# Split attention and a max-out FFN on one core: one ring of four PSUM banks, V loaded by half sequence, masks by a compare, a regrouped first FFN chunk

## The chip, the cores and the metric

The kernel runs on one core of a Trainium2 chip. TensorE (PE in the profile) multiplies matrices and transposes; its weight loads are listed apart as PEld. VectorE (DVE), ScalarE (ACT) and GpSimd (POOL) do elementwise work; In this kernel whatever leaves PSUM goes through DVE or ACT. SyncE (SP) issues most DMAs. The metric is device time in microseconds, the median of several executions of the whole kernel. Every engine works through its own instructions strictly in program order, and semaphores tie the engines together: an instruction that waits holds back all that stands behind it on its engine.

## The reference

Attention over 4 batches, 8 heads, 768 positions and a head width of 64, followed by a feed-forward network (FFN) with a maximum of three projections. Some heads ("retrieval" heads, by a flag in the input) see all earlier positions; the others see the first 4 positions and a window of 64.

```python
scores = q @ k.T / sqrt(64)                   # per batch and head, 768 x 768
mask = causal if is_retrieval[h] else causal & (first 4 positions | last 64)
a = softmax(where(mask, scores, -1e9))
x = (a @ v)  -> [4*768, 8*64]                 # heads side by side
h = maximum(maximum(x @ w1, x @ w2), x @ w3)  # 512 -> 768
out = h @ w_out                               # 768 -> 512, float32
```

## The kernel before, in words

The work is cut into 32 steps. Step `s` is one batch, one half of the sequence (384 query positions) and one pair of heads; four steps in a row (the four head pairs) make one half, eight steps one batch. A step of the first half has 6 blocks of 128x128 scores a head, a step of the second half has 15. The instructions are issued in the order in which the Python loop writes them (`manual_schedule`); no planner moves them.

For each step the loop does this, and the names in brackets are those of the profile:

- `load(s)`: SP loads K, Q and V of the step (`ks`, `qs`, `vs`), seven steps ahead.
- `prep(s)`: DVE casts K to fp16 (`kn`, L268), ACT casts Q (`qn`, L269). `prep_v(s)`: V is cast into a store of all heads (`va`, by ACT in the first four steps, by DVE later, L281), and POOL writes a second store `vf` (L283) in which the far positions of non-retrieval heads are zeroed.
- `turn(s)`: PE transposes K and Q into one PSUM tile (`tr`, L296), DVE copies it out (`KQ`, L303).
- `scores(s, units)`: PE multiplies K by Q into PSUM (`st`, two buffers of two banks each, L324), ACT takes the exponential (`pt`, L334), POOL multiplies the blocks on the diagonal and next to it by masks (`mk`, L356). A first-half step has two units, a second-half step four: `[0, 1]` at the step's start, `[2, 3]` later in it.
- `av(s)`: PE multiplies the exponentials by V (`oacc`, L371; a column of ones in V gives the softmax sum); DVE takes the reciprocal (`rc`, L379) and multiplies (`x`, L381).
- `turn_x(s)`: PE transposes `x` (`tr`, L396), DVE copies it out (`xT`, L399).

When the four head pairs of a half are done, `ffn(b, half)` is queued. It is a generator of 24 units. Eighteen units are four matmuls each over 384 positions into PSUM (`yy`, L219), for six blocks of the 768 columns and three weights: the first weight's product is copied by ACT into `acc` (L227), the second and the third are compared with it by DVE (`acc`, then `hT`, L230). The last six units are three products with `w_out` (`yy`, L237; each is counted as two), copied by ACT (`ot`, L244) and stored by SP (L246). The units of one half are spread over the steps that follow it: `share` issues some of them at three points of every step. The last half's units have no steps left and stand at the end.

PSUM has eight banks. Before the change four belong to `st`, one to `oacc`, one to `tr` (shared by `turn` and `turn_x`), two to `yy`. A tile that takes a buffer of its pool waits until the reader of that buffer's last tile has finished. `yy` therefore waits for the reader of the `yy` two units earlier; `tr` waits for the copy of the `tr` before it.

The masks `mk` of the eight heads are built at the start, per head pair, by a DVE instruction with two SBUF inputs (L175). The seven loads of the weights are issued by POOL after step 1.

Of the kernel before, what the change touches and what calls it, by code (L numbers as in the profile page):

```python
# [48 lines left out]
def kernel(  # L49
# [54 lines left out]


    staged = {}

    def load(s):
        b, half, hp = where(s)
        hs, ts = slice(2 * hp, 2 * hp + 2), slice(half * HALF, (half + 1) * HALF)  # L110
        t = []
        for nm, src in (("ks", k), ("qs", q), ("vs", v)):
            st = stage.tile([P, 2, HB, D], FP32, tag=nm, name=nm)
            if nm == "vs":
                for hl in range(2):
                    nc.sync.dma_start(
                        out=st[:, hl],
                        in_=src[b, 2 * hp + hl, ts].rearrange("(j p) d -> p j d", p=P),
                    )
            else:  # L120
                nc.sync.dma_start(
                    out=st, in_=src[b, hs, ts].rearrange("h (p j) d -> p h j d", p=P)
                )
            t.append(st)
        staged[s] = t

    ir32 = consts.tile([P, 2 * H], mybir.dt.int32, name="ir32")
# [4 lines left out]
    for s in range(AHEAD):  # L132
        load(s)
# [14 lines left out]
    W = consts.tile([P, 512], FP16, name="W")  # L148
    nc.gpsimd.affine_select(
        out=W[:, 0:256], in_=base, compare_op=ALU.is_gt, fill=0.0,  # L150
# [4 lines left out]
    nc.vector.tensor_copy(out=W[:, 256:512], in_=W[:, 0:256])  # L155
    if n_sink > 0:
        nc.vector.tensor_copy(out=W[0:n_sink, 256:512], in_=base[0:n_sink, :])
    F = consts.tile([P, 512], FP16, name="F")
    for c in (0, 256):
        nc.vector.tensor_tensor(  # L160
            out=F[:, c : c + 256], in0=base, in1=W[:, c : c + 256], op=ALU.subtract
        )
    RT = consts.tile([P, H], FP32, name="RT")
    nc.vector.tensor_copy(out=RT, in_=ir32[:, 0 : 2 * H : 2])

    far = consts.tile([P, H, 4], FP16, name="far")
    nc.vector.tensor_copy(out=far, in_=RT.unsqueeze(2).to_broadcast([P, H, 4]))
    if n_sink > 0:
        nc.vector.memset(far[0:n_sink, :, 0:1], 1.0)

    mk = consts.tile([P, H, 512], FP16, name="mk")

    def head_masks(hp):
        for h in (2 * hp, 2 * hp + 1):
            nc.vector.scalar_tensor_tensor(  # L175
                out=mk[:, h], in0=F, scalar=RT[:, h : h + 1], in1=W,
                op0=ALU.mult, op1=ALU.add,
            )

# [4 lines left out]

    w_t = [consts.tile([P, KS, DF], FP16, name=f"w{wi}t") for wi in range(3)]
    woutt = consts.tile([P, NNB, DMdl], FP16, name="woutt")

    def load_weights():
        for c in (0, DF // 2):
            for wt, w in zip(w_t, (moe_w1, moe_w2, moe_w3)):  # L190
                nc.gpsimd.dma_start(
                    out=wt[:, :, c : c + DF // 2],
                    in_=w[:, c : c + DF // 2].rearrange("(ks p) n -> p ks n", p=P),
                )
        nc.gpsimd.dma_start(
            out=woutt, in_=moe_w_out.rearrange("(ns p) m -> p ns m", p=P)
        )
# [4 lines left out]
    def ffn(b, half):  # L202
# [3 lines left out]
        def psum():  # L206
            nonlocal n_yy
            n_yy += 1
            if last and n_yy % 2:
                return sps.tile([P, 2, 512], FP32, tag="st", name="yst")[:, 0, :]  # L210
            return fsp.tile([P, 512], FP32, tag="fsp", name="yy")

        hT = [htp.tile([P, HALF], FP16, tag=f"hT{n}", name=f"hT{n}") for n in range(NNB)]
        for ni in range(NNB):
            acc = None
            for wi in range(3):
                yy = psum()
                for ks in range(KS):
                    nc.tensor.matmul(  # L219
                        yy[:, 0:HALF],  # L220
                        w_t[wi][:, ks, ni * P : (ni + 1) * P],
                        xT[b, half][ks],
                        start=(ks == 0), stop=(ks == KS - 1),
                    )
                if wi == 0:
                    acc = fwork.tile([P, HALF], FP16, tag="acc", name="acc")
                    nc.scalar.copy(out=acc, in_=yy[:, 0:HALF])  # L227
                else:
                    dst = acc if wi == 1 else hT[ni]
                    nc.vector.tensor_tensor(  # L230
                        out=dst, in0=yy[:, 0:HALF], in1=acc, op=ALU.max
                    )
                yield
# [30 lines left out]
    def prep(s):  # L264
        qs, ks_ = staged[s][1], staged[s][0]
        qn = half16.tile([P, HB, 2, D], FP16, tag="qn", name="qn")
        kn = half16.tile([P, HB, 2, D], FP16, tag="kn", name="kn")
        nc.vector.tensor_copy(out=kn, in_=ks_.rearrange("p h j d -> p j h d"))  # L268
        nc.scalar.copy(out=qn, in_=qs.rearrange("p h j d -> p j h d"))  # L269
        cast[s] = (kn, qn)  # L270

    def prep_v(s):
        b, half, hp = where(s)
        vs = staged.pop(s)[2]
# [3 lines left out]
        if s < NHP:  # L278
            nc.scalar.copy(out=vdst, in_=vs)
        else:  # L280
            nc.vector.tensor_copy(out=vdst, in_=vs)  # L281
        k1 = min(k0 + HB, 4)
# [8 lines left out]
    def turn(s):  # L291
        tr = trp.tile([P, 1024], FP16, tag="tr", name="tr")
# [17 lines left out]
    def scores(s, us):  # L310
# [21 lines left out]
        for u, st in zip(us, sts):  # L332
# [4 lines left out]
            for at, u0, nu, cols, n, m0 in MASKED[half]:  # L337
                if at != u:
                    continue
                for hl_all in (slice(0, 2),):  # L340
# [15 lines left out]
                    nc.gpsimd.tensor_tensor(out=x, in0=x, in1=m, op=ALU.mult)  # L356
# [3 lines left out]
    def av(s):  # L360
        b, half, hp = where(s)
        pt, j = pts.pop(s), b % 2
        o = ops.tile([P, HB, 2, VW], FP32, tag="oacc", name="oacc")
# [23 lines left out]
    def turn_x(s):  # L387
# [6 lines left out]
        tr = trp.tile([P, 1024], FP16, tag="tr", name="tr")  # L394
# [8 lines left out]

    FIRST = NHP + 1
    weight = [0 if s < FIRST else (5, 7)[where(s)[1]] for s in range(NSTEP)] + [3]
    units = (2 * B - 1) * 24
    emitted = 0

    def share(s, part, parts):
        nonlocal emitted  # L410
        if s > NSTEP:
            return
        want = units * (sum(weight[:s]) + weight[s] * (part + 1) / parts) / sum(weight)
        n = int(want + 1e-6) - emitted
        if n > 0:
            fill(n)
            emitted += n

    head_masks(0)
    prep(0)  # L420
    turn(0)
    head_masks(1)
    prep(1)
    prep_v(0)
    for s in range(NSTEP + 2):
# [62 lines left out]
```

## Time and profile before

| | |
|---|---|
| median of 3 runs | 243.78 us (243.57 to 244.28) |
| the profiled execution | 244.76 us, of which the span of the profile is 243.1 us |
| PE busy | 206.3 us (85%), weight loads 122.2 us (50%) |
| DVE / ACT / POOL busy | 147.4 (61%) / 132.0 (54%) / 128.5 us (53%) |
| granted TensorE clock | 1.0 throughout |
| moved by DMA | 28.65 MB, mean 118 GB/s |

Three stretches follow each other in the profile: a start in which the first five steps run without any FFN (until 35 us), the body in which steps and FFN units alternate (until about 222 us), and the end with the last half's FFN alone. In the answers quoted below a row of a timeline gives the start in microseconds, how long the group took, engine, line, operation, what it writes and reads, the number of instructions, and in square brackets how long the engine stood idle before it and what ended that.

### The profile page before, as it was taken

The numbers are of one execution on the slowest core, as the hardware profiler recorded it, in microseconds if no ns is written. First come the engines' busy times: TensorE is split into PE (matmuls) and PEld (weight loads), VectorE is DVE, ScalarE is ACT, GpSimd is POOL, SyncE is SP. The second block draws the span as 40 slices with busy tenths as digits, with TensorE's granted clock in tenths as the row PEclk, the third lists the DMA queues.
The fourth block names the chain that finished last, engine by engine and source line by source line (L and its number), as shares of the span: only waits on it lengthen the run. The fifth ranks groups of instructions, "written<-read, shape, count | busy, mean of one in ns | idle before, by whom it ended". The sixth has DMA issues, their size and how long they took to land.

```text
span 243.1 us, 5176 instructions
## 1 busy us (share of the span) xinstructions
PE 206.3 (85%) x2000; PEld 122.2 (50%) x2000; DVE 147.4 (61%) x302; ACT 132.0 (54%) x206; POOL 128.5 (53%) x144
## 2 busy tenths in 40 slices
PE   0455389999998999898988999898989999889993
PEld 0234256655654555564645555564545455555551
DVE  4696545665587736755687546764787646542550
ACT  3564273675643486656644497465535676643222
POOL 2599981655776455437776264528775166441000
PEclk9999999999999999999999999999999999999999
DMA  5999999951892039102783059003300020002103
GB/s 149 282 281 250 207 214 217 253 131 49 253 260 62 3 118 266 39 0 74 230 228 90 3 171 251 3 0 113 116 4 0 27 106 0 3 0 89 46 0 129
DMA packets 50584, 28.65 MB, mean 118 GB/s; under 512 B 27264, under 2 KB 47488, under 8 KB 50560
## 3 DMA queue, kind: packets, MB, share of 16 engines
q1 hardware_dynamic: 46464, 25.18, 37.8%
q0 software_dynamic: 3952, 3.15, 8.1%
q8 instruction: 15, 0.25, 0.4%
q14 instruction: 9, 0.07, 0.1%
q10 hardware_dynamic: 144, 0.01, 0.0%
HBM read 25.17 MB, written 6.29 MB: 129 GB/s over the span
## 4 chain that ended last, share of the span: by engine, by line
PE 48%; DVE 16%; ACT 9%; POOL 9%; issue 8%; DMA 6%; SPq 3%; POOLq 0%; DVEq 0%; ACTq 0%
PE yy L219 19%; PE yy L237 9%; POOL pt L356 7%; PE oacc L371 7%; ACT pt L334 6%; PE st L324 4%; DVE kn L268 4%; DMA ks<-in_k_dram 3%; PE tr L296 3%; DVE acc L230 3%; PE yst L219 2%; DMA qs<-in_q_dram 2%; DVE va L281 2%; DVE mk L175 2%; ACT acc L227 2%
## 5 line engine op out<-in xcount | busy, mean ns | idle before, releaser
L356 POOL TENSOR_TENSOR pt<-pt,mk 128x512 f16<-128x512 f16 (+1 forms) x96 | 101.6, 1081 | 78.4 <-ACT pt L334 78.3
L334 ACT ACTIVATE pt<-st 128x1024 f16<-128x1024 f32 x96 | 83.0, 918 | 42.7 <-PE st L324 34.6
L230 DVE TENSOR_TENSOR acc<-yy,acc 128x384 f16<-128x384 f32 x45 | 25.0, 555 | 26.9 <-PE yy L219 13.5
L219 PE MATMUL yy<-xT,w0t 128*128 128x384 f16 x180 | 37.7, 330 | 3.8 <-DVE acc L230 3.6
L219 PE MATMUL yy<-xT,w2t 128*128 128x384 f16 x180 | 37.2, 330 | 4.2 <-ACT acc L227 4.2
L219 PE MATMUL yy<-xT,w1t 128*128 128x384 f16 x180 | 37.3, 330 | 2.5 <-ACT acc L227 1.7
L227 ACT CAST acc<-yy 128x384 f16<-128x384 f32 x45 | 21.7, 482 | 32.5 <-PE yy L219 28.1
L303 DVE COPY KQ<-tr 128x768 f16<-128x768 f16 x32 | 30.5, 954 | 14.0 <-PE tr L296 14.0
L324 PE MATMUL st<-KQ 64*128 64x384 f16 (+2 forms) x320 | 29.9, 297 | 4.9 <-DVE KQ L303 3.6
L237 PE MATMUL yy<-woutt,hT 128*128 128x512 f16 x132 | 32.5, 379 | 0.5 <-DVE acc L230 0.4
L371 PEld LDWEIGHTS <-pt 128*128 128x128 f16 x672 | 26.3, 100 | 7.2 <-POOL pt L356 3.5
L371 PE MATMUL oacc<-va,pt 128*128 128x65 f16 x352 | 26.7, 199 | 2.9 <-POOL pt L356 2.8
L230 DVE TENSOR_TENSOR hT<-yy,acc 128x384 f16<-128x384 f32 x45 | 25.0, 555 | 5.8 <-PE yy L219 3.5
L283 POOL TENSOR_TENSOR vf<-va,far 128x390 f16<-128x390 f16 (+1 forms) x32 | 20.7, 648 | 11.9 <-DVE va L281 6.0
L219 PEld LDWEIGHTS <-w2t 128*128 128x128 f16 x192 | 17.9, 98 | 16.0 <-issue 6.9
L219 PEld LDWEIGHTS <-w1t 128*128 128x128 f16 x192 | 17.9, 98 | 15.6 <-issue 6.4
L219 PEld LDWEIGHTS <-w0t 128*128 128x128 f16 x192 | 17.8, 99 | 14.9 <-issue 5.7
L244 ACT COPY ot<-yy 128x512 f32<-128x512 f32 x22 | 13.1, 594 | 21.2 <-PE yy L237 21.2
L399 DVE COPY xT<-tr 128x384 f16<-128x384 f16 x32 | 11.4, 356 | 19.9 <-PE tr L396 19.6
L296 PE MATMUL tr<-ident,kn 128*128 128x128 f16 x96 | 11.7, 237 | 13.4 <-DVE kn L268 8.1
L324 PEld LDWEIGHTS <-KQ 64*128 64x128 f16 x320 | 11.9, 98 | 20.3 <-issue 11.2
L371 PE MATMUL oacc<-vf,pt 128*128 128x65 f16 x320 | 21.7, 194 | 0.0
(44 smaller groups left out, 165.4 us busy)
## 6 DMA issues: line engine op xcount, KB each, us to landing
ks<-in_k_dram SPq DMA_DIRECT2D x32, 192.0 KB, 4.0
qs<-in_q_dram SPq DMA_DIRECT2D x32, 192.0 KB, 4.1
vs<-in_v_dram SPq DMA_DIRECT2D x64, 96.0 KB, 3.9
out_dram<-ot SPq DMA_DIRECT2D x24, 256.0 KB, 2.1
w0t<-in_moe_w_dram POOLq DMA_DIRECT2D x2, 384.0 KB, 10.9
w1t<-in_moe_w_dram POOLq DMA_DIRECT2D x2, 384.0 KB, 13.0
w2t<-in_moe_w_dram POOLq DMA_DIRECT2D x2, 384.0 KB, 15.2
woutt<-in_moe_w_out_dram POOLq DMA_DIRECT2D x1, 768.0 KB, 23.2
```

The lines of the kernel that those rows point to most:

```text
L219: nc.tensor.matmul(yy[:, 0:HALF], w_t[wi][:, ks, ni * P : (ni + 1) * P], xT[b, half][ks], start=(ks == 0), stop=(ks == KS - 1),)
L227: nc.scalar.copy(out=acc, in_=yy[:, 0:HALF])
L230: nc.vector.tensor_tensor(out=dst, in0=yy[:, 0:HALF], in1=acc, op=ALU.max)
L237: nc.tensor.matmul(yo[:, 0:DMdl], hT[ns][:, tb * P : (tb + 1) * P], woutt[:, ns, :], start=(ns == 0), stop=(ns == NNB - 1),)
L244: nc.scalar.copy(out=ot, in_=yo[:, 0:DMdl])
L283: nc.gpsimd.tensor_tensor(out=vf[j][:, hs, k0:k1, 0 : D + 1], in0=va[j][:, hs, k0:k1, 0 : D + 1], in1=far[:, hs, k0:k1].unsqueeze(3).to_br ...
L296: nc.tensor.transpose(tr[:, c : c + P], x[:, j].rearrange("p h d -> p (h d)"), ident)
L303: nc.vector.tensor_copy(out=KQs[s].rearrange("p (i t j) -> p i t j", i=2, j=HB), in_=tr[:, 0:S].rearrange("p (i j t) -> p i t j", i=2, j=HB),)
L324: nc.tensor.matmul(st[:, hl, c0 : c0 + n * P], KT[ki // HB if half else 0][hb : hb + D, ki % HB * P : (ki % HB + 1) * P], KQ[hb : hb + D, ...
L334: nc.scalar.activation(out=pt[:, u, :, 0:w], in_=st[:, :, 0:w], func=AF.Exp, scale=sc)
L356: nc.gpsimd.tensor_tensor(out=x, in0=x, in1=m, op=ALU.mult)
L371: nc.tensor.matmul(o[:, qi, hl, 0 : D + 1], pt[:, u, hl, c : c + P], vv[:, 2 * hp + hl, ki, 0 : D + 1], start=(idx == 0), stop=(idx == len ...
```

## The change

1. **PSUM.** The pools of `oacc`, `tr` and `yy` become one pool of four banks (`bank(...)`) that is taken in turn: every new `tr`, `oacc` or `yy` waits for the reader of the tile four places earlier in program order. `st` keeps its four banks. `acc` gets a pool of seven buffers.
2. **Order within a step.** `share` issues its units after `turn_x`, after `av` and at the step's end (before: after `turn_x`, between `turn` and `av`, at the end). In steps 1 to 4 `turn_x` of the step before comes right after `av` in the same step, ahead of the next scores. The 24 units of a half are now dealt out over exactly four steps: 5, 5, 6, 8 units in the steps 9 to 12 and 6, 6, 7, 5 in the steps 13 to 16, and so on (before: about 5 in a first-half step, 7 in a second-half step).
3. **V.** One group of three DMAs of 256 KB loads V of all eight heads for one half (at the load of its second head pair), instead of two DMAs of 96 KB in every step. In the first four steps ACT issues the DMAs of Q.
4. **Masks.** One tile `kept` holds 0, 1 or 2 for every place; a head's mask is `kept > least`, a compare with one SBUF input (L197). In the first four steps the mask of unit 1 is applied by DVE, no longer by POOL. The flags and masks come after the first `turn`.
5. **First FFN.** `ffn(0, 0)` runs by weight: six blocks with `w1`, six with `w2`, six with `w3`. The weights are loaded whole, one in each of the steps 0 to 3, in four DMAs.
6. `vf` is written for one block in the first half and three in the second (before three and one).

The diff, cut to what the prediction speaks of:

```diff
+    accp = ctx.enter_context(tc.tile_pool(name="accp", bufs=7))
-    ops = ctx.enter_context(tc.tile_pool(name="ops", bufs=1, space=bass.MemoryType.PSUM))
-    trp = ctx.enter_context(tc.tile_pool(name="trp", bufs=1, space=bass.MemoryType.PSUM))
-    fsp = ctx.enter_context(tc.tile_pool(name="fsp", bufs=2, space=bass.MemoryType.PSUM))
+    bkp = ctx.enter_context(tc.tile_pool(name="bkp", bufs=4, space=bass.MemoryType.PSUM))
+    def bank(shape, dtype, name):
+        return bkp.tile(shape, dtype, tag="bank", name=name)
...
-        for nm, src in (("ks", k), ("qs", q), ("vs", v)):
+        for nm, src in (("ks", k), ("qs", q)):
+            eng = nc.scalar if s < NHP and nm == "qs" else nc.sync
...
+        if hp == 1:
+            vs = stage.tile([P, H, HB, D], FP32, tag="vs", name="vs", bufs=3)
+            for j in range(HB):
+                r0 = half * HALF + j * P
+                nc.sync.dma_start(
+                    out=vs[:, :, j], in_=v[b, :, r0 : r0 + P].rearrange("h p d -> p h d")
+                )
...
-            nc.vector.scalar_tensor_tensor(
-                out=mk[:, h], in0=F, scalar=RT[:, h : h + 1], in1=W,
-                op0=ALU.mult, op1=ALU.add,
-            )
+            nc.vector.tensor_scalar(
+                out=mk[:, h], in0=kept, scalar1=least[:, h : h + 1], scalar2=None,
+                op0=ALU.is_gt,
+            )
...
+        order = [(wi, ni) for ni in range(NNB) for wi in range(3)]
+        if (b, half) == (0, 0):
+            order.sort()
+        for wi, ni in order:
+            yy = psum()
...
-                    nc.gpsimd.tensor_tensor(out=x, in0=x, in1=m, op=ALU.mult)
+                    eng = nc.vector if s < NHP and u == 1 else nc.gpsimd
+                    eng.tensor_tensor(out=x, in0=x, in1=m, op=ALU.mult)
...
-        if s > 1:
+        if s > FIRST:
             turn_x(s - 2)
-        share(s, 1, 7)
+        share(s, 0, 3)
         if s + 1 < NSTEP:
             turn(s + 1)
-        share(s, 3, 7)
         if 0 < s <= NSTEP:
             av(s - 1)
+        if 0 < s < FIRST:
+            turn_x(s - 1)
+        share(s, 1, 3)
         if s + 2 < NSTEP:
             prep(s + 2)
         if live and n_u > 2:
             scores(s, [2, 3])
         if s + 1 < NSTEP:
             prep_v(s + 1)
-        if s + 2 < NHP:
-            head_masks(s + 2)
-        share(s, 6, 7)
-        if s == 1:
-            load_weights()
+        if 0 < s < NHP - 1:
+            head_masks(s + 1)
+        share(s, 2, 3)
+        if s < 4:
+            load_weight(s)
```

Where the instructions move is seen in three places. The first is DVE at the start, from the first `kn` on. Before:

```order
L268 CAST kn<-ks 128x384
L303 COPY KQ<-tr 128x768
L175 SCALAR_TENSOR_TENSOR mk<-F,RT,W 128x512 x2
L268 CAST kn<-ks 128x384
L303 COPY KQ<-tr 128x768
L268 CAST kn<-ks 128x384
L175 SCALAR_TENSOR_TENSOR mk<-F,RT,W 128x512 x2
L303 COPY KQ<-tr 128x768
```

With the change:

```order
L197 TENSOR_SCALAR mk<-kept,least 128x512 x2
L376 TENSOR_TENSOR pt<-pt,mk 128x2x256
L322 COPY KQ<-tr 128x768
L287 CAST kn<-ks 128x384
L376 TENSOR_TENSOR pt<-pt,mk 128x2x256
L322 COPY KQ<-tr 128x768
L399 RECIPROCAL rc<-oacc 128x6
L401 TENSOR_TENSOR x<-oacc,rc 128x384
L419 COPY xT_266<-tr 128x384
```

A mask product on `pt` (it waits for the exponentials of its step) now stands ahead of the copy `KQ` for the next step's scores.

The second place is ACT at the start. Before:

```order
L128 DMA ir_96<-in_is_retrieval_dram 128x16
L138 ACT_TABLE_LOAD
L138 ACTIVATE warm<-warm 128x2
L269 CAST qn<-qs 128x384 x2
L279 CAST va_171<-vs 128x2x3x64
L334 ACTIVATE pt<-st 128x1024
```

With the change:

```order
L120 DMA qs<-in_q_dram 128x2x192
L136 DMA ir_97<-in_is_retrieval_dram 128x16
L120 DMA qs<-in_q_dram 128x2x192 x3
L146 ACT_TABLE_LOAD
L146 ACTIVATE warm<-warm 128x2
L288 CAST qn<-qs 128x384 x2
L298 CAST va_147<-vs 128x2x3x64
L353 ACTIVATE pt<-st 128x1024
```

The cast `va` of step 0 stands ahead of the first exponential in both; with the change it reads a `vs` that three DMAs of 256 KB fill, the third of which is the fifth DMA on SP.

The third place is DVE in a first-half step of the body (step 10, from its `xT` on). Before:

```order
L399 COPY xT_1105<-tr 128x384
L230 TENSOR_TENSOR hT_1015<-yy,acc 128x384
L303 COPY KQ<-tr 128x768
L379 RECIPROCAL rc<-oacc 128x6
L381 TENSOR_TENSOR x<-oacc,rc 128x384
L268 CAST kn<-ks 128x384
L281 CAST va_172<-vs 128x2x3x64
L230 TENSOR_TENSOR acc<-yy,acc 128x384
L230 TENSOR_TENSOR hT_1016<-yy,acc 128x384
```

With the change:

```order
L419 COPY xT_1065<-tr 128x384
L249 TENSOR_TENSOR hT_974<-yy,acc 128x384
L322 COPY KQ<-tr 128x768
L399 RECIPROCAL rc<-oacc 128x6
L401 TENSOR_TENSOR x<-oacc,rc 128x384
L249 TENSOR_TENSOR acc<-yy,acc 128x384
L249 TENSOR_TENSOR hT_975<-yy,acc 128x384
L287 CAST kn<-ks 128x384
L300 CAST va_148<-vs 128x2x3x64
```

The two maxima, which free banks of `yy`, now stand ahead of the casts `kn` and `va`, which free none.

More of the change, by code (lines that the diff above doesn't have):

```diff
@@ L131 @@
     )
-    for s in range(AHEAD):
+    for s in range(1, AHEAD):
         load(s)
@@ L273, in prep_v @@
         b, half, hp = where(s)
[L274 removed]
+        vs = staged_v[b, half]
         j, k0 = b % 2, half * HB
@@ L362, in av @@
         pt, j = pts.pop(s), b % 2
-        o = ops.tile([P, HB, 2, VW], FP32, tag="oacc", name="oacc")
+        o = bank([P, HB, 2, VW], FP32, "oacc")
         todo = [
@@ L404 @@
     FIRST = NHP + 1
-    weight = [0 if s < FIRST else (5, 7)[where(s)[1]] for s in range(NSTEP)] + [3]
-    units = (2 * B - 1) * 24
-    emitted = 0
     def share(s, part, parts):
-        nonlocal emitted
-        if s > NSTEP:
+        if s < FIRST or s > NSTEP:
             return
[L413 to L419, printed above, removed]
+        s0 = s - (s - FIRST) % NHP
+        ws = [(5, 7, 6)[where(i)[1] if i < NSTEP else 2] for i in range(s0, s0 + NHP)]
+        at = s - s0
+        before, now = (
+            24 * (sum(ws[:at]) + ws[at] * x / parts) / sum(ws) for x in (part, part + 1)
+        )
+        if (part, at) == (parts - 1, NHP - 1):
+            now = 24
+        fill(int(now + 1e-6) - int(before + 1e-6))
     prep(0)
     turn(0)
+    head_flags()
+    head_masks(0)
+    prep(1)
     head_masks(1)
-    prep(1)
     prep_v(0)
```

130 lines of the change are left out of this document (66 added, 64 removed).

## The prediction

> **What bounds the kernel now.** I read first the page's busy times, then the table of windows: one batch of the body, and the body from step 9 on.
>
> ```profile
> PE 206.3 (85%) x2000; PEld 122.2 (50%) x2000; DVE 147.4 (61%) x302; ACT 132.0 (54%) x206; POOL 128.5 (53%) x144
> ...
> 74.82:128.30 53.48, 49.47 (x500) 29.18 (x500) 34.52 (x72) 31.89 (x50) 30.02 (x33) 1.00 0.41 117
> 63.40:221.90 158.50, 145.99 (x1480) 86.27 (x1479) 101.47 (x213) 92.20 (x144) 87.02 (x93) 1.00 0.31 90
> ```
>
> The window's columns are length, then PE, weight loads, DVE, ACT and POOL with their instructions, granted clock, DMA share, GB/s. A batch of eight steps takes 53.48 us; the body holds 158.5/53.48 = 2.96 of them. PE is the busiest engine, but the busy time overstates pipelined matmuls, so I take start-to-start distances from PE's timeline: a second-half step that begins without a stall, then the kinds of stall.
>
> ```profile
> 95.66 0.61 PE L324 MATMUL st<-KQ 64*128 64x384 f16 x8
> 96.21 0.34 PE L396 MATMUL tr<-ident,x 128*128 128x128 f16 x3
> 96.39 0.81 PE L219 MATMUL yy<-xT,w2t 128*128 128x384 f16 x4
> 97.03 0.81 PE L219 MATMUL yy<-xT,w0t 128*128 128x384 f16 x4
> 97.69 0.33 PE L296 MATMUL tr<-ident,kn 128*128 128x128 f16 x3
> ...
> 98.02 0.81 PE L219 MATMUL yy<-xT,w1t 128*128 128x384 f16 x4
> ...
> 99.32 0.23 PE L371 MATMUL oacc<-vf,pt 128*128 128x65 f16 x2
> ...
> 100.35 0.55 PE L324 MATMUL st<-KQ 64*128 64x384 f16 x6
> 100.84 0.82 PE L219 MATMUL yy<-xT,w0t 128*128 128x384 f16 x4
> ...
> 102.94 0.81 PE L219 MATMUL yy<-xT,w2t 128*128 128x384 f16 x4 [0.62 <-ACT acc L227]
> ...
> 72.87 0.81 PE L219 MATMUL yy<-xT,w2t 128*128 128x384 f16 x4
> 74.82 0.48 PE L219 MATMUL yy<-xT,w0t 128*128 128x384 f16 x2 [1.14 <-DVE acc L230]
> ...
> 112.39 0.50 PE L324 MATMUL st<-KQ 64*128 64x384 f16 x6
> 112.82 0.34 PE L396 MATMUL tr<-ident,x 128*128 128x128 f16 x3
> 113.61 0.33 PE L296 MATMUL tr<-ident,kn 128*128 128x128 f16 x3 [0.45 <-DVE xT L399]
> ```
>
> One FFN unit costs PE 0.65 (96.39 to 97.03); an output product, six matmuls of 512 columns instead of four of 384, 0.65 x 6/4 x 512/384 = 1.30. A second-half step's attention costs 0.55 (95.66 to 96.21) + 0.18 + 0.33 (97.69 to 98.02) + 1.03 (99.32 to 100.35) + 0.49 = 2.58. A first-half step has 0.43 (112.39 to 112.82) for scores, the same transposes, and 12 instead of 30 value products, 0.41: 1.35. A batch is 36 x 0.65 + 6 x 1.30 + 4 x 2.58 + 4 x 1.35 = 46.9. So PE loses 6.6 of 53.48 us, nearly all of it waiting for a bank: `yy` for the reader two units back (102.94 instead of 102.14; 74.82 instead of 73.52), `tr` for the copy of the `tr` before (113.61 instead of 113.00).
>
> **The change part by part.** *The ring.* Behind 74.82 stands this piece of DVE's timeline:
>
> ```profile
> 71.54 0.95 DVE L303 COPY KQ<-tr 128x768 f16<-128x768 f16 x1
> 72.42 0.20 DVE L379 RECIPROCAL rc<-oacc 128x6 f32<-128x6 f32 x1
> 72.65 0.56 DVE L381 TENSOR_TENSOR x<-oacc,rc 128x384 f16<-128x384 f32 x1
> 73.12 0.54 DVE L268 CAST kn<-ks 128x384 f16<-128x384 f32 x1
> 73.58 0.72 DVE L281 CAST va<-vs 128x384 f16<-128x384 f32 x1
> 74.22 0.54 DVE L230 TENSOR_TENSOR acc<-yy,acc 128x384 f16<-128x384 f32 x1
> ```
>
> The maximum that frees the bank stood behind `kn` and `va`, 1.26 us. It now stands ahead of them, and the bank is asked for two tiles later. These stalls go; what is late next I find by walking a step with the rows above and these means of one batch:
>
> ```profile
> L230 DVE TENSOR_TENSOR hT<-yy,acc 128x384 f16<-128x384 f32 x12 | 6.6, 554 | 1.3 <-PE yy L219 0.9
> L281 DVE CAST va<-vs 128x384 f16<-128x384 f32 x8 | 3.2, 402 | 0.0
> L399 DVE COPY xT<-tr 128x384 f16<-128x384 f16 x8 | 2.9, 356 | 5.0 <-PE tr L396 5.0
> L334 ACT ACTIVATE pt<-st 128x1024 f16<-128x1024 f32 x16 | 16.0, 1028 | 8.2 <-PE st L324 5.5 <-POOL vf L283 1.4 <-POOL pt L356 1.3
> L227 ACT CAST acc<-yy 128x384 f16<-128x384 f32 x12 | 5.8, 484 | 7.4 <-PE yy L219 7.4
> L269 ACT CAST qn<-qs 128x384 f16<-128x384 f32 x8 | 4.2, 521 | 0.0
> L334 ACT ACTIVATE pt<-st 128x768 f16<-128x768 f32 x4 | 3.2, 807 | 0.0
> L356 POOL TENSOR_TENSOR pt<-pt,mk 128x512 f16<-128x512 f16 x20 | 22.9, 1152 | 21.4 <-ACT pt L334 21.4
> ```
>
> *First-half steps.* DVE does `xT`, `KQ`, `rc`, `x`, `kn`, `va` = 0.36 + 0.95 + 0.20 + 0.56 + 0.54 + 0.40 = 3.0, and two maxima for every three units. Steps 9 and 10 have 5 units: 3.0 + 1.85 and, as an estimate, 0.25 between ten instructions = 5.1, against PE's 1.35 + 3.25 = 4.6. DVE becomes their bound: 5.1 and 5.1, with 6 units 5.5. Step 16 has mostly output products, which ACT copies: PE's 4.6 and a little, 4.9.
>
> *Second-half steps.* Here ACT comes to bind. Scores need a pair of banks that the exponential two units back has read. With two units behind `[2, 3]` (1.3 us; before, three) the next step's scores are there before the last exponential (0.81) is through, and wait. From those scores on PE does the rest of them 0.3, transposes 0.18, two units 1.3, `tr` 0.33, `oacc` 1.03, two units 1.3 = 4.4; ACT then casts `acc` (0.48) and `qn` (0.52) ahead of the exponentials, 1.03 and 0.81. With 0.8 between the step's first two score units, a period of 7.4 comes out, where PE's own work with 6 units is 2.58 + 3.9 = 6.5. Steps 13 and 14 take 7.4 each; step 15, 7 units, 8.0; step 12, 8 units, PE's 7.8.
>
> The batch becomes 5.1 + 5.1 + 5.5 + 7.8 + 7.4 + 7.4 + 8.0 + 4.9 = 51.2, 2.3 less; over 2.96 batches **-6.8**. Bounds: 47.5 a batch if all stalls but small gaps go, 53.5 if DVE and ACT hold PE as before.
>
> *The start.* Rows of the first steps, the price of a DVE product, and the first window:
>
> ```profile
> 9.05 1.51 ACT L334 ACTIVATE pt<-st 128x1024 f16<-128x1024 f32 x2 [0.71 <-PE st L324]
> ...
> 12.63 0.82 PE L324 MATMUL st<-KQ 64*128 64x384 f16 x6 [1.05 <-DVE KQ L303]
> 28.01 1.04 PE L324 MATMUL st<-KQ 64*128 64x384 f16 x8
> 35.05 1.48 PE L219 MATMUL yy<-xT,w0t 128*128 128x384 f16 x4
> ...
> L160 DVE TENSOR_TENSOR F<-base,W 128x256 f16<-128x256 f16 x2 | 0.5, 272 | 0.0
> ...
> 0.00:10.00 10.00, 1.64 (x12) 0.84 (x12) 6.00 (x16) 3.87 (x7) 3.02 (x10) 1.00 0.78 201
> ```
>
> Ahead of ACT's first exponential stands `va`, which now needs V of all heads, 768 KB, with 6 x 192 KB of K and Q on the way: 1.9 MB, at the first window's 201 GB/s 9.6 us. `va` then ends near 10.2 and the exponentials near 11.8, 1.2 later than now. Behind them stand the mask on DVE (two pieces like L160, 0.55; at most POOL's 1.15) and `KQ`: scores of step 1 at about 13.6 instead of 12.63. From there each step is a chain: 0.65 from scores to exponentials (as at 12.63), both 1.51, mask 0.55, `KQ` 0.95, `rc` and `x` 0.76, transposes 0.5 = 4.9. Step 4 comes at 13.6 + 3 x 4.9 = 28.3, now 28.01. The old head masks and the queue of seven weight loads leave DVE and POOL; I count nothing, since the chain does not pass through them. From step 4 to the first FFN unit I keep the 7.0 of the rows. **+0.3**, between -3 and +4.
>
> One row speaks against a mask on DVE: POOL's `vf` took 1.27 while DVE built masks, 0.83 without.
>
> ```profile
> 8.42 1.27 POOL L283 TENSOR_TENSOR vf<-va,far 128x390 f16<-128x390 f16 x1 [5.86 <-DVE KQ L303]
> 13.00 0.83 POOL L283 TENSOR_TENSOR vf<-va,far 128x390 f16<-128x390 f16 x1
> ```
>
> The Trainium skill (SBUF — State Buffer, "Who interferes with whom") says that a DVE instruction with two SBUF inputs contends with a GpSimd instruction that reads SBUF and that the later one waits; by that rule the mask would wait too, and the sum would be higher by up to the rows' 0.44 in each of four steps, 1.8 us.
>
> *The rest.* The first FFN by weight gives ACT six casts in step 5: 3 x 1.03 + 0.81 + 0.52 + 6 x 0.48 = 7.3, no more than the 7.4 above; DVE gets six maxima in steps 6 and 7: 3.0 + 3.3 = 6.3, hidden under the same. 0. `vf` changes places between the halves: 0, since POOL is idle 23 of 53 us. The last FFN keeps its own order: 0. V's DMAs move the same bytes under a body with a DMA share of 0.31; without that cover each group would cost like the first, 1.2.
>
> Sum against the profiled execution: 244.76 - 6.8 + 0.3 = 238.3. The median lies 0.98 below that execution: **237 us**.
>
> **The rivals.** *The ring frees everything* (0.17): 47.5 a batch, -17.7 in all: 226. For it: DVE and ACT are busy only 34.5 and 31.9 us of a batch. Against it: the walk meets both at fixed points of every step.
>
> *PE waits for POOL's masks* (0.13, slower): `oacc` now stands two units, 1.3 us, closer behind the scores `[2, 3]`, whose last two masks take 2.3 behind the exponential of unit 2. PE has 0.49 + 1.3 + 0.55 + 0.18 + 1.3 + 0.33 = 4.15 from those scores to `oacc`; exponential and masks need 0.35 + 1.03 + 2.3 = 3.7. The margin is 0.45. Were the masks slowed as `vf` was (1.27/0.83), they would take 1.2 more, and PE would wait 0.8 in each of four steps: the batch is 51.2 + 3.2 = 54.4, and the sum 244.76 + 0.9 x 2.96 + 0.3 - 0.98 = 247. It decides from 2.3/4 = 0.6 a step, where the gain is gone.
>
> *The limits stay* (0.08): ACT and DVE, not the banks, already hold PE, and the batch stays at its 53.48: 244. Against it: the two stalls above end at the reader of a bank two units back.
>
> *The start pays* (0.07): the bound of +4 is due: 237 + 3.7 = 241; with half the body's gain as well, no gain is left.
>
> The forecast, 231 to 242 by itself: 0.55.
>
> **How the numbers follow.** A measurement of this kernel tells about 0.3%, 0.7 us, from no change. Faster: 0.55 + 0.17 + 0.05 of the start's case = 0.77; same 0.08; slower 0.13 + 0.02 = 0.15. The range leaves out most of the slower case and the best of the ring: 227 to 244.
>
> **What would show it.** `yy` waiting for ACT's `acc` should vanish from PE's waits, `st` waiting for the exponentials appear, some 0.5 in each second-half step. A batch should take 51.2, first-half steps 5.1 with DVE hardly idle. The first exponential should start near 10.2, the first FFN unit near 35.4. I am wrong if PE waits for `KQ`, `x` or masks inside the body, if a batch takes under 49 or over 53, or if the first FFN unit comes past 38.

## The result, and the profile after

The changed kernel takes **235.78 us** (median of 4 runs, 235.46 to 235.96) against 244.03 us (243.57 to 245.13) of the kernel before beside it: a ratio of **0.965, with a 95% interval of 0.962 to 0.969**. The profiled execution took 235.46 us, its span 233.7 us, 9.4 less than the span before (243.1).

From the page of the kernel after, the busy times and the shares of the engines in the chain of work that ended last:

```profile
PE 203.3 (87%) x2000; PEld 120.8 (52%) x2000; DVE 144.2 (62%) x306; ACT 131.2 (56%) x206; POOL 121.0 (52%) x137
...
PE 68%; ACT 11%; POOL 3%; issue 3%; DVE 2%; POOLq 0%; ACTq 0%; DVEq 0%
```

The busy times changed little; the largest fall is POOL's, 7.5 us. PE stood idle 36.8 us of the span before (243.1 less 206.3) and 30.4 us after. PE's table of waits gives what it waited for, microseconds in all, how often, and the longest. The waits for a bank in the kernel before:

```profile
PE yy L219 <- ACT acc L227: 5.9, 12, 0.7
PE tr L296 <- DVE xT L399: 5.4, 6, 2.7
PE yy L219 <- DVE acc L230: 3.6, 4, 1.1
```

The kernel after, over its whole span:

```profile
PE tr L416 <- DVE x L401: 8.4, 4, 2.6
PE st L343 <- DVE KQ L322: 7.3, 2, 6.2
PE tr L315 <- DVE kn L287: 5.5, 4, 4.6
PE st L343 <- ACT pt L353: 3.6, 10, 0.8
```

No `yy` is in it any more, and no `tr` that waits for the copy `xT`. The first three rows are all of the start. The fourth is of the body, but for its longest wait (0.8, at 37.04): nine times 0.31 us in second-half steps, `st` waits for the exponentials.

To see where the 9.4 us come from, I cut both spans at the scores of a step on PE's timeline. The scores of steps 16 to 24 in the kernel after (start, length, then as before) give the length of each step:

```profile
110.46 0.50 PE L343 MATMUL st<-KQ 64*128 64x384 f16 x6
115.32 0.50 PE L343 MATMUL st<-KQ 64*128 64x384 f16 x6
120.10 0.50 PE L343 MATMUL st<-KQ 64*128 64x384 f16 x6
124.76 0.50 PE L343 MATMUL st<-KQ 64*128 64x384 f16 x6
130.07 0.61 PE L343 MATMUL st<-KQ 64*128 64x384 f16 x8
...
137.56 0.39 PE L343 MATMUL st<-KQ 64*128 64x384 f16 x4
...
144.82 0.40 PE L343 MATMUL st<-KQ 64*128 64x384 f16 x4
145.52 0.39 PE L343 MATMUL st<-KQ 64*128 64x384 f16 x4 [0.31 <-ACT pt L353]
...
151.97 0.40 PE L343 MATMUL st<-KQ 64*128 64x384 f16 x4
...
160.33 0.50 PE L343 MATMUL st<-KQ 64*128 64x384 f16 x6
```

A batch now takes 160.33 - 110.46 = 49.87 us instead of the 53.48 of the prediction's first window. The steps are 4.86, 4.78, 4.66, 5.31 and 7.49, 7.26, 7.15, 8.36.

The start went the other way. Rows of the kernel after, from ACT, DVE and PE in turn:

```profile
11.69 0.51 ACT L298 CAST va<-vs 128x384 f16<-128x384 f32 x1 [3.26 <-DMA vs<-in_v_dram]
...
13.64 0.99 DVE L376 TENSOR_TENSOR pt<-pt,mk 128x512 f16<-128x512 f16 x1 [4.67 <-ACT pt L353]
...
15.55 0.82 PE L343 MATMUL st<-KQ 64*128 64x384 f16 x6 [6.22 <-DVE KQ L322]
...
20.36 0.50 PE L416 MATMUL tr<-ident,x 128*128 128x128 f16 x3 [2.58 <-DVE x L401]
20.80 0.82 PE L343 MATMUL st<-KQ 64*128 64x384 f16 x6
...
31.34 1.04 PE L343 MATMUL st<-KQ 64*128 64x384 f16 x8
...
38.29 2.74 PE L238 MATMUL yy<-xT,w0t 128*128 128x384 f16 x8
```

`va` waits for V until 11.69; the mask takes 0.99 in front of `KQ`; step 1 comes at 15.55, and each step takes 5.25 from there (15.55, 20.80). Step 4 is reached at 31.34 instead of 28.01, the first FFN unit at 38.29 instead of 35.05. So the sum is **+3.2 us in the start and -12.6 from the first FFN unit on** (233.7 - 38.29 = 195.4 against 243.1 - 35.05 = 208.0). The second part holds 2.96 batches of 3.6 = 10.7, and 1.2 of the steps 5 to 8 (38.29 to 65.45 is 27.2; before, 35.05 to 63.38, 28.3); the rest, 0.7, lies in step 9, which took 6.23 us before (63.38 to 69.61) where the same step a batch later took 5.51 (117.57 to 123.08).

### The profile page after: what moved, and what is told of

Read it like the earlier page. It is cut to its first block, busy times and chain, and to the rows that moved or that the text cites. A ratio compares the mean times of both kernels' runs of the same rounds, so it can differ in the third digit from the quotient of the medians.

```text
span 233.7 us, 5102 instructions
## 1 busy us (share of the span) xinstructions
PE 203.3 (87%) x2000; PEld 120.8 (52%) x2000; DVE 144.2 (62%) x306; ACT 131.2 (56%) x206; POOL 121.0 (52%) x137
## 4 chain that ended last, share of the span: by engine, by line
PE 68%; ACT 11%; POOL 3%; issue 3%; DVE 2%; POOLq 0%; ACTq 0%; DVEq 0%
PE yy L238 34%; ACT pt L353 9%; PE oacc L391 8%; PE yy L256 8%; PE st L343 6%; PE tr L315 4%; POOL pt L376 3%; PE tr L416 3%; PE yst L238 3%; ACT qn L288 1%; PE yst L256 1%; DVE KQ L322 1%; DVE x L401 0%; POOLq L507 0%; DVE pt L376 0%
## 5 line engine op out<-in xcount | busy, mean ns | idle before, releaser
L376 POOL TENSOR_TENSOR pt<-pt,mk 128x512 f16<-128x512 f16 (+1 forms) x92 | 97.3, 1078 | 64.4 <-ACT pt L353 64.2
L343 PE MATMUL st<-KQ 64*128 64x384 f16 (+2 forms) x320 | 31.2, 297 | 11.3 <-DVE KQ L322 7.3
L322 DVE COPY KQ<-tr 128x768 f16<-128x768 f16 x32 | 30.4, 951 | 10.6 <-PE tr L315 10.6
L238 PE MATMUL yy<-xT,w1t 128*128 128x384 f16 x180 | 36.2, 326 | 0.0
L238 PE MATMUL yy<-xT,w2t 128*128 128x384 f16 x180 | 36.1, 326 | 0.0
L302 POOL TENSOR_TENSOR vf<-va,far 128x130 f16<-128x130 f16 (+1 forms) x32 | 20.0, 625 | 23.9 <-DVE va L300 14.2
L256 PE MATMUL yy<-woutt,hT 128*128 128x512 f16 x132 | 31.0, 379 | 0.0
L419 DVE COPY xT<-tr 128x384 f16<-128x384 f16 x32 | 11.4, 356 | 30.4 <-PE tr L416 30.4
L343 PEld LDWEIGHTS <-KQ 64*128 64x128 f16 x320 | 13.1, 98 | 32.5 <-issue 20.3
L391 PEld LDWEIGHTS <-pt 128*128 128x128 f16 x672 | 25.5, 100 | 1.6 <-POOL pt L376 1.2
L238 PEld LDWEIGHTS <-w1t 128*128 128x128 f16 x192 | 17.3, 97 | 11.8 <-issue 2.4
L256 PEld LDWEIGHTS <-hT 128*128 128x128 f16 x144 | 13.3, 98 | 14.6 <-issue 0.6
```

Of the source, the lines that this page charges most:

```text
L238: nc.tensor.matmul(yy[:, 0:HALF], w_t[wi][:, ks, ni * P : (ni + 1) * P], xT[b, half][ks], start=(ks == 0), stop=(ks == KS - 1),)
L256: nc.tensor.matmul(yo[:, 0:DMdl], hT[ns][:, tb * P : (tb + 1) * P], woutt[:, ns, :], start=(ns == 0), stop=(ns == NNB - 1),)
L302: nc.gpsimd.tensor_tensor(out=vf[j][:, hs, k0:k1, 0 : D + 1], in0=va[j][:, hs, k0:k1, 0 : D + 1], in1=far[:, hs, k0:k1].unsqueeze(3).to_br ...
L322: nc.vector.tensor_copy(out=KQs[s].rearrange("p (i t j) -> p i t j", i=2, j=HB), in_=tr[:, 0:S].rearrange("p (i j t) -> p i t j", i=2, j=HB),)
L343: nc.tensor.matmul(st[:, hl, c0 : c0 + n * P], KT[ki // HB if half else 0][hb : hb + D, ki % HB * P : (ki % HB + 1) * P], KQ[hb : hb + D, ...
L376: eng.tensor_tensor(out=x, in0=x, in1=m, op=ALU.mult)
```

## The experiments: the ring and the order

Theory after the result: the ring frees PE in the body, the loads of V and the masks on DVE lose in the start. Ring and order were made apart first, which with the two kernels gives a table of four.

**Without the ring:**

```diff
-        return bkp.tile(shape, dtype, tag="bank", name=name)
+        return {"tr": trp, "oacc": ops, "yy": fsp}[name].tile(shape, dtype, tag=name, name=name)
```

> The changed kernel, with the ring undone: one bank for tr, one for oacc, two for yy, as before; order, deal of units, V and masks as in the change. Theory (the ring is what the body gains by): yy waits for its reader two units back and tr for the copy of the tr before, as in the kernel before; a batch goes back to 53 us, the time to 235.8 + 2.96 x 3.2 = 245. Rival (the order, maxima ahead of kn and va and even portions of units, is what pays): a batch stays under 51, the time under 239.

Measured: 243.46 us, 0.995 of before (0.993 to 0.997). Nearly all of the gain goes with the ring; the batch, shown below, is 52.27 where the theory said 53.

**The ring alone,** on the kernel before (its `ops`, `trp` and `fsp` become one pool of four banks, nothing else):

> The kernel before, with the ring of four banks alone; nothing else of the change. Theory (the ring pays by itself): the waits of yy and tr go, a batch falls from 53.5 to 50.5, the time to 244 - 3 x 3.0 = 235; the start keeps its first FFN unit at 35.05. Rival (the ring needs the new order): the maxima still stand behind kn and va, a batch stays over 52.5, the time over 241.

Measured: 229.48 us, 0.940 of before (0.938 to 0.942): better than the whole change by 6 us, and better than the 235 expected. Of the 6.2 us between the two spans, 3.3 lie in the start (the first FFN unit comes at 34.98, not 38.29) and 2.9 behind it. One batch (scores of step 16 to scores of step 24) in the windows of, in turn, the kernel without the ring, the ring alone and the whole change; the columns are those of the prediction's first windows, whose 53.48 is the batch of the kernel before:

```profile
114.17:166.44 52.27, 49.41 (x503) 29.02 (x502) 34.56 (x72) 31.80 (x50) 29.98 (x33) 1.00 0.45 121
```

```profile
106.43:155.10 48.67, 48.01 (x502) 29.10 (x502) 34.13 (x72) 31.90 (x50) 30.03 (x33) 1.00 0.46 130
```

```profile
110.46:160.33 49.87, 48.69 (x501) 29.05 (x501) 34.55 (x72) 31.73 (x50) 29.96 (x33) 1.00 0.48 127
```

Every engine does the same work in all of them; only the length differs. The ring alone takes 4.8 off a batch, the rest of the change without the ring 1.2, and that rest on top of the ring **adds** 1.2; the next two runs show that it is the order that adds it. In the ring's kernel the maxima still stand behind `kn` and `va` on DVE, and yet PE's table of waits has no wait for `acc` or for the copies of `tr` in that batch; its one row is 0.5 us for `hT`, which the output product reads. Four banks cover what the old order makes late. So the order was no part of the gain.

**The old order in the changed kernel:** `share` at its three old points and with its old portions, the rest as changed.

```diff
-        ws = [(5, 7, 6)[where(i)[1] if i < NSTEP else 2] for i in range(s0, s0 + NHP)]
...
+    weight = [0 if s < FIRST else (5, 7)[where(s)[1]] for s in range(NSTEP)] + [3]
+        share(s, 3, 7)
         if 0 < s <= NSTEP:
             av(s - 1)
-        share(s, 1, 3)
```

> The changed kernel, with the order and the deal of the FFN units put back: share between turn and av again, at the three points and with the weights 5 and 7 over the whole kernel, as before; the ring, V, masks, the first FFN and the early turn_x of the change stay. Theory (the new order costs the body, since the scores of a second-half step come two units behind [2, 3] and wait for the exponential): the waits of st for pt (3.6 us in all) fall to about 0.8, a batch goes from 49.87 to the 48.7 of the ring alone, the time from 235.8 to about 232. Rival (the ring alone is quicker for its start only): a batch stays at 49.9 and the time within 0.3% of 235.8.

Measured: 232.35 us, 0.949 (0.946 to 0.952); the batch is 48.67 (108.79 to 157.46), as with the ring alone, and `st` waits for `pt` 0.8 us in the whole span. As the theory had it; but this undoes the deal and the place together.

**Only the place:** the middle group of units goes back between `turn` and `av`, the new deal stays.

```diff
         if s + 1 < NSTEP:
             turn(s + 1)
+        share(s, 1, 3)
         if 0 < s <= NSTEP:
             av(s - 1)
...
-        share(s, 1, 3)
```

> The changed kernel, with only the middle group of FFN units put back between turn and av; the deal of 24 units over four steps, in thirds of each step, stays. It tells apart the two halves of the order, which the run with the old order undid together. Theory (the deal costs: second-half steps with 6 units have two behind [2, 3] and the next scores come too soon for the exponential): st still waits for pt three times a batch, 0.9 us, a batch stays near 49.9, the time near 235.8. Rival (the place of the middle group costs, maxima ahead of kn and va): the batch goes to 48.7, the time to 232.

Measured: 230.90 us, 0.945 (0.942 to 0.949); the batch is 48.47. My theory (the deal) was wrong and the rival right: the place of one group costs the 1.4 us a batch. ACT shows why. A second-half step with 6 units in the changed kernel (its scores start at 144.82):

```profile
150.10 0.48 ACT L246 CAST acc<-yy 128x384 f16<-128x384 f32 x1 [2.43 <-PE yy L238]
150.47 0.52 ACT L288 CAST qn<-qs 128x384 f16<-128x384 f32 x1
150.89 2.64 ACT L353 ACTIVATE pt<-st 128x1024 f16<-128x1024 f32 x3
```

and the same step with the group in its old place (scores at 142.70):

```profile
146.65 0.48 ACT L246 CAST acc<-yy 128x384 f16<-128x384 f32 x1 [1.15 <-PE yy L238]
147.03 0.52 ACT L288 CAST qn<-qs 128x384 f16<-128x384 f32 x1
147.92 1.73 ACT L353 ACTIVATE pt<-st 128x1024 f16<-128x1024 f32 x2 [0.38 <-PE st L343]
```

Behind `av`, the group's `yy` reaches ACT 150.10 - 144.82 = 5.28 us into the step; between `turn` and `av` it is 3.95. ACT stands idle 2.43 for it, with `qn` and the exponentials of `[2, 3]` queued behind that cast. With the group in its old place they start 5.22 instead of 6.07 into the step, and the next scores find their bank free: PE's table has no wait at all in that batch. Of the 1.4 us, 1.3 lie in the four second-half steps (130.07 to 160.33 above is 30.26; here 28.97).

**The first FFN in the order of the others:**

```diff
-        if (b, half) == (0, 0):
-            order.sort()
```

> The changed kernel, with the first FFN in the order of the others (three weights for each block) and its whole weights as in the change. The prediction put this part at 0: time 235.8, within 0.7. Rival (the third weight comes late): it is issued at 24.8 us and lands 11 us later, near 36, and the first unit that needs it stands 1.3 us behind the first FFN unit, near 39.6: no wait either, unless the landing slips by 4 us; then up to 4 us slower.

Measured: 236.17 us, 0.967 (0.964 to 0.970), span 233.7 as with the change. This part is worth nothing here.

## The experiments: the start

**V of the first half per head pair:**

```diff
+        if s < NHP:
+            vp = stage.tile([P, 2, HB, D], FP32, tag="vp", name="vp", bufs=NHP)
+            for hl in range(2):
+                nc.sync.dma_start(
+                    out=vp[:, hl],
+                    in_=v[b, 2 * hp + hl, ts].rearrange("(j p) d -> p j d", p=P),
+                )
```

> The changed kernel, with V of the first half loaded per head pair again (two DMAs of 96 KB in each of the first four steps); all later V as in the change. Theory (the first exponential waits for V of all heads): the first cast va starts near 8.5 us instead of 11.69, the scores of step 1 come near 12.5 instead of 15.55, the chain of 5.25 us a step stays, the first FFN unit moves from 38.29 to about 35.5, and the time falls by about 2.8 us, 1.2%. Rival (the chain is set by something later, the weights or POOL): va comes earlier but step 4 stays near 31.3, and the time within 0.3% of the changed kernel's 235.8.

Measured: 233.40 us, 0.955 (0.950 to 0.959). Its rows on ACT and PE:

```profile
7.09 0.51 ACT L306 CAST va<-vp 128x384 f16<-128x384 f32 x1
8.85 1.51 ACT L361 ACTIVATE pt<-st 128x1024 f16<-128x1024 f32 x2 [1.25 <-PE st L351]
...
12.98 0.82 PE L351 MATMUL st<-KQ 64*128 64x384 f16 x6 [2.29 <-DVE KQ L330]
...
28.75 1.04 PE L351 MATMUL st<-KQ 64*128 64x384 f16 x8
```

The exponentials start at 8.85, not 12.11; step 4 comes 2.6 us earlier, the step of 5.25 stays. The theory holds.

**`turn_x` of the first steps late again:**

```diff
-        if s > FIRST:
+        if s > 1:
             turn_x(s - 2)
...
-        if 0 < s < FIRST:
-            turn_x(s - 1)
```

> The changed kernel, with turn_x of steps 0 to 3 where it was before (two steps later, behind the scores). Theory (PE stands for x, 2.4 us in each early step, with the next scores behind it): a step of the start becomes scores to exponentials 0.65, exponentials 1.5, mask 1.0, KQ 0.95, in all 4.1 instead of 5.25; step 4 comes 3.5 us earlier, near 27.8, the first FFN unit near 35.3, and the time falls by about 3 us to 233. Rival (POOL's masks set the pace, since the value products stand ahead of the scores): the wait moves to the value products and the time stays within 0.3%.

**All masks of the first steps on POOL** (`eng = nc.gpsimd`):

> The changed kernel, with all masks of the first four steps on POOL again. Theory (the mask in front of KQ on DVE is a part of the chain): KQ starts as soon as its transposes are done; POOL becomes the pace with 2.9 of masks, 0.4 of vf and 0.85 of a weight load, 4.2 a step instead of 5.25; step 4 near 28.2, first FFN unit near 35.5, time 233. Rival (POOL holds the value products, and x behind them, longer than the DVE mask held KQ): step 4 at 31.3 or later, time 235.8 or more.

Measured: 230.53 us, 0.944 (0.940 to 0.949), and 230.86 us, 0.944 (0.941 to 0.948). With `turn_x` late the steps take 4.1, 4.4 and 4.4, and the first FFN unit comes at 33.99; with POOL's masks they take 5.0, 4.7 and 4.1, from an earlier step 1 (13.04, since `KQ` no longer waits behind a mask), and it comes at 33.74. For both I expected 233; the first FFN units come 1.3 and 1.8 us earlier than said, and the times are 2.5 and 2.1 better. Each takes out the same chain at another place, `KQ` behind a mask or the scores behind `x`.

**All masks of the first steps on DVE** (`eng = nc.vector if s < NHP else nc.gpsimd`):

> The changed kernel, with all three masks of the first four steps on DVE, so that POOL makes none. It measures the price of a mask on DVE with POOL at rest. Theory A (a mask on DVE is slow because POOL's masks run beside it): each takes about 0.55, as two pieces of the first 128x256 product (0.29); three take 1.65, a step of the start 5.25 + 0.65 = 5.9, time 237. Theory B (the form costs it, POOL or not): each takes about 0.99, three 3.0, a step 7.2, time 241.

Measured: 233.51 us, 0.955 (0.952 to 0.958). Three masks now take what one took. DVE in step 1 of this kernel, then POOL and DVE in step 1 of the changed kernel:

```profile
16.73 0.96 DVE L376 TENSOR_TENSOR pt<-pt,mk 128x512 f16<-128x512 f16 x3 [1.30 <-ACT pt L353]
```

```profile
17.32 1.96 POOL L376 TENSOR_TENSOR pt<-pt,mk 128x512 f16<-128x512 f16 x2 [0.91 <-ACT pt L353]
...
17.75 1.00 DVE L376 TENSOR_TENSOR pt<-pt,mk 128x512 f16<-128x512 f16 x1 [1.79 <-ACT pt L353]
```

A mask takes DVE 0.32 with POOL at rest and 1.00 beside POOL's masks, which keep their 0.98. Theory A holds in its cause, and the price is lower than it said: I had 0.55 from twice a product of half the width. The step of the start becomes 4.7 and not the 5.9 of the expectation, the time 233.5 and not 237.

**Three edits of the start together,** V per pair, `turn_x` late, masks on DVE:

> The changed kernel with three edits of its start together: V of the first half per head pair, turn_x of steps 0 to 3 two steps later, all masks of the first four steps on DVE with POOL at rest (three took 0.96 us together in the run before). Theory (each takes its own piece of one chain): exponentials of step 0 at 8.85, scores of step 1 near 11.6, a step of 3.6 us, step 4 near 22.4, the first FFN unit 5.6 later, near 28; time 235.8 - 10 = 226. Rival (the DMAs become the bound: K and Q of the steps and 3.1 MB of weights at about 270 GB/s): steps wait for ks, first FFN unit near 31, time 229 or more.

Measured: 235.57 us, 0.965 (0.961 to 0.969): no gain at all on the changed kernel. The steps do take 3.6 to 3.9, and step 4 comes at 23.46. Then DVE, ACT and PE stand:

```profile
32.72 0.36 DVE L308 CAST va<-vs 128x384 f16<-128x384 f32 x1 [8.17 <-DMA vs<-in_v_dram]
...
33.84 0.51 ACT L296 CAST qn<-qs 128x384 f16<-128x384 f32 x1 [7.79 <-DMA qs<-in_q_dram]
...
35.33 1.31 PE L351 MATMUL st<-KQ 64*128 64x384 f16 x8 [8.24 <-ACT pt L361]
...
36.87 1.17 PE L246 MATMUL yy<-xT,w0t 128*128 128x384 f16 x3
```

The rival was right that the DMAs become the bound (229 or more), though V and Q came late and not K, and the first FFN unit came at 36.87 and not near 31. V of the second half is three DMAs of 256 KB whose issue alone took SP from 12.35 to 23.65, beside the weights that POOL had issued from 11.56 on; SP issued the next K and Q behind them, and the exponentials for which PE stood are behind the cast `qn` of such a Q.

**All of it with the ring, the old order and V per pair in every step:**

> The ring with the old order and deal (as in the kernel before), V per head pair in every step, turn_x two steps later, masks by the compare, those of the first four steps on DVE, weights whole in the steps 0 to 3, the first FFN by weight. Theory: a step of the start takes 3.7 us, V of step 4 is 192 KB and not 768, so nothing waits 8 us for it; step 4 near 23.5, first FFN unit near 30, 4 to 5 us ahead of the ring alone (34.7); body as with the ring alone; time 225. Rival (the DMAs, busy 99% from 8 to 40 us, set the start): kn or va wait for K, Q or V, or the first FFN unit for its weights, it comes no earlier than 34, and the time stays at 229 or more.

Measured: 223.49 to 233.00 us in four runs, which is no result to compare; in the profiled one (233.00) PE again stood 8.19 us, for `kn` and `qn` whose DMAs came late. One DMA of K was 4.3 us in its issue (15.36 to 19.65), while the weights were under way.

**The same with the weights later:**

```diff
-        if s < 4:
-            load_weight(s)
+        if s in (1, 3, 4, 5):
+            load_weight((1, 3, 4, 5).index(s))
```

> The version of the run before (ring, old order, V per head pair, turn_x two steps later, masks of the first steps on DVE), with the four weight loads at the ends of the steps 1, 3, 4 and 5 instead of 0 to 3. Theory (the weights, 2.4 MB issued between 11.6 and 19.1 us, hold back K and Q of the steps 6 and 7, and PE stands 8.2 us): kn and qn wait no more than 1 us in steps 4 and 5, step 5 comes near 28.5, the first FFN unit near 29.5, the body follows as with the ring alone (from first unit to end 192.5 us): time 223.5, with little spread. Rival (the DMAs cannot carry K, Q, V and one weight by 29 us in any order): the wait moves to the first or the seventh FFN unit, for w0t or w1t, or stays at kn; time 228 or more.

Measured: **223.19 us** (221.72 to 223.72), **0.914 of before (0.911 to 0.916)**, the best version of this study, and the 223.5 of the theory. PE in its start:

```profile
23.53 1.03 PE L342 MATMUL st<-KQ 64*128 64x384 f16 x8 [1.24 <-DVE KQ L321]
...
27.95 0.40 PE L342 MATMUL st<-KQ 64*128 64x384 f16 x4 [0.80 <-ACT pt L352]
...
29.16 1.58 PE L237 MATMUL yy<-xT,w0t 128*128 128x384 f16 x8
```

No wait for K, Q or V is left in the steps 4 and 5, and the first FFN unit comes 9.1 us earlier than in the changed kernel (38.29). The bytes are the same; only which of them come first differs. One of the four runs with the early weights took 223.49 as well, the other three 228.89 or more; the six here lie between 221.72 and 223.72. So the later weights are shown to keep the time steady, as far as four and six runs can show it, not to beat the best run with the early ones. The new deal with the old place (batch of 48.47) was not put into this version.

## Why the prediction was right, and where its steps were not

The time (235.78 against 237) and its sign came out within the forecast. On the spans the prediction summed -6.5, and -9.4 was measured, from two terms that were mis-sized against each other: the body gained 5.8 us more than summed, the start lost 2.9 more. That the time came out within 1.2 us is in part luck.

- **The ring, -6.8, measured -12.6 from the first FFN unit on.** The mechanism was right: waits for `yy` and for the `tr` copy are gone. Of the missing 5.8, a batch's 51.2 that was 49.87 makes 3.9 (2.96 x 1.33), and the steps 5 to 8, which I had left at nothing, 1.2; 0.7 lies in step 9.
- **First-half steps "bound by DVE", 5.1, 5.1, 5.5, 4.9 (20.6 in all), measured 4.78, 4.66, 5.31, 4.86 (19.6).** This step failed. I added up DVE's durations and put 0.25 for gaps on top. In the trace of after DVE's instructions start before the one ahead has ended:

```profile
69.58 0.56 DVE L249 TENSOR_TENSOR hT<-yy,acc 128x384 f16<-128x384 f32 x1
70.06 0.54 DVE L287 CAST kn<-ks 128x384 f16<-128x384 f32 x1
70.52 0.35 DVE L300 CAST va<-vs 128x384 f16<-128x384 f32 x1
70.78 0.55 DVE L249 TENSOR_TENSOR acc<-yy,acc 128x384 f16<-128x384 f32 x1
71.25 0.34 DVE L419 COPY xT<-tr 128x384 f16<-128x384 f16 x1
```

  From 69.58 to 71.25 are four instructions of 2.00 by their durations, in 1.67: some 0.08 less for each, where I had put 0.03 more. With that DVE needs 4.85 - 0.8 = 4.1 a step, and PE's 4.6 binds, as the rows show (4.66 without a wait).
- **"PE loses 6.6 of 53.48", from a PE time of 46.9 a batch.** This PE time was too low. With the place put back a batch takes 48.47 us with no wait in PE's table, so the waits were worth 5.0, and the best batch measured stays 1.0 above the bound of 47.5.
- **Second-half steps "bound by ACT's exponentials", 7.8, 7.4, 7.4, 8.0 (30.6), measured 7.49, 7.26, 7.15, 8.36 (30.3).** Right in place and nearly in size: `st` waits 0.31 in three of four, where I said 0.5. The terms of the period shown for it (4.4, 0.48, 0.52, 1.03, 0.81) add up to 7.2, not 7.4, which is nearer to the 7.26 and 7.15 measured. I named two causes, the units behind `[2, 3]` and ACT's casts ahead of the exponentials; the run with only the place put back shows that the casts' lateness is the one that counts.
- **"The maximum now stands ahead of `kn` and `va`, and the bank is asked for two tiles later."** I let both carry the gain. The runs give it to the ring alone (48.67), and the order on top took 1.2 a batch back. The rival that the ring frees everything (47.5 a batch, 226) was nearer to the ring by itself (48.67, 229.5) than my walk was.
- **The start, +0.3, measured +3.2.** Two of its terms failed. `va` was to end near 10.2, behind 1.9 MB at 201 GB/s, and ended near 12.2. The rate held: over the first 11.69 us of the kernel after the DMAs moved 199 GB/s. That is 2.3 MB: 0.4 MB more than I had counted moved ahead of V's end. The scores of step 1 came 1.95 later than said (15.55 for 13.6). The mask was 0.99, not 0.55, and each step 5.25, not 4.9: three steps, 1.05. From step 4 to the first FFN unit the 7.0 kept from the rows was right (6.95). My own mark "wrong if the first FFN unit comes past 38" was reached. The rule of the Trainium skill (SBUF — State Buffer, "Who interferes with whom") that I weighed and priced at up to 0.44 a mask but left out of the sum agrees with the runs: the mask took 0.32 with POOL at rest and 0.99 beside POOL's masks. That 0.99 is just 0.44 above my 0.55 is luck, since the price itself is 0.67 over 0.32. The 0.44 also came from a misread row: at 13.00, where `vf` took 0.83, DVE was building masks as well.

```profile
12.95 2.09 DVE L175 SCALAR_TENSOR_TENSOR mk<-F,RT,W 128x512 f16<-128x512 f16 x2
```

- **First FFN by weight, 0:** right, as measured. **Queues, `vf` between halves, the end, 0:** nothing in the traces speaks against it; they were not tried apart.
- **PE waits for POOL's masks (247):** did not happen; PE waited for them 0.4 us, once in the whole span, at 210.29 in the value products of the last step. The slowing of POOL's masks that it priced (1.27/0.83) rests on the same misread row.

## What to carry to other kernels

Put PSUM tiles with different readers into one ring before moving instructions: here the ring alone was worth 6%, and the hand-made order on top lost part of it. When a kernel's start has a chain over four engines, look at the order of the DMAs as well: single cuts of the chain paid here (230.53 and 230.86), but with three together, from 5.25 us a step to between 3.6 and 3.9, the gain was lost to a stand of 8.24 us for late DMAs. A stand of that length is in the traces of both versions with the cut chain and early weights, and not in that with later ones. Do not add up the durations of one engine's queue where the trace shows starts: distances from start to start are the price.

## What the runs showed of the hardware

- A DVE product with two SBUF inputs took 0.32 us with POOL at rest and 1.00 beside POOL's products, which kept 0.98 each. A compare with a single SBUF input, two of which take 0.61 us alone, took 1.52 beside them in the run with V per pair:

```profile
9.73 1.52 DVE L205 TENSOR_SCALAR mk<-kept,least 128x512 f16<-128x512 f16 x2
...
9.95 1.82 POOL L384 TENSOR_TENSOR pt<-pt,mk 128x512 f16<-128x512 f16 x2 [0.75 <-ACT pt L361]
```

  So the compare of the change is not free of it either. The same section of the Trainium skill (SBUF — State Buffer, "Who interferes with whom") has this too, for instructions of that kind when they run in a mode with two ports; the trace does not show the mode.
- After the start of the changed kernel, which is full of waits, PE runs at about half its later rate in the first FFN units: eight matmuls of 384 columns take 2.74 us at 38.29 in the changed kernel (row above) and 1.46 at 42.18, though the granted clock is recorded as 1.00 there (a row of PE's timeline, then a window of PE: length, busy time with instructions, granted clock, DMA share, GB/s):

```profile
42.18 1.46 PE L238 MATMUL yy<-xT,w0t 128*128 128x384 f16 x8
```

```profile
36.00:42.00 6.00, 5.12 (x49) 1.00 1.23 227
```

  In the run that stood 8.24 us the record shows it as well:

```profile
36.00:42.00 6.00, 5.22 (x40) 0.50 1.02 175
```

  In the best version, whose start keeps PE busier (15.0 us of the 24 from 6 to 30, against 9.4 in the changed kernel), the first eight matmuls take 1.58 (at 29.16). So a slow start can cost again behind it, here 1.3 us in eight matmuls (2.74 against 1.46). Late `turn_x` has 1.58 there too, with PE busy 10.7 of the 24, so busy time over the start alone does not settle it; what does is open.
- Issuing a DMA itself took long in places: SP's issue of three V DMAs took 11.3 us in the run with three edits, against 3.3 in the changed kernel at about the same place (11.69). In the changed kernel itself the next three, issued from 20.98 on, took until 35.90. That the weights were the cause is shown only in so far as the waits went with their later issue.
